# Two blocks as one unit in a Strassen feed-forward: 256 moving rows in the first layer, one load of the second layer's leaves for both

## The chip, the cores and the metric

The kernel runs on one core of one Trainium2 chip. The metric is the device time of one execution in microseconds (us); three runs of the kernel before the change took 1131.85, 1136.12 and 1137.38 us, the median is 1136.12.

## What is computed

Random-feature attention on 8 x 8 heads of 576 rows of 64, then, on its output put together as 4608 rows of 512, a Fourier mix and a feed-forward part, all in float32:

```python
q_p, k_p = (phi(q_s), phi(k_s))              # phi: exp(h - max h) of 128 features
kv = np.einsum('bhsm,bhsd->bhmd', k_p, v)
num = np.einsum('bhsm,bhmd->bhsd', q_p, kv)  # attn_out = num / den
...
u = x + np.real(fft(fft(x, axis=1), axis=2))
un = (u - mean(u)) / np.sqrt(var(u) + 1e-06)
ch = np.maximum(un @ w_ch1, 0.0) @ w_ch2     # 512 -> 2048 -> 512
return u + ch
```

## The kernel before

**Two stages.** The first 423 us hold attention, the Fourier mix, the weights' preparation and the feed-forward of the first 512 rows (four plain blocks of 128). The rest is the feed-forward of eight blocks of 512 rows, numbered j = 0 to 7, and only this is changed.

**A block** is two layers, `un @ w_ch1` (`first_of`, L1466) and `hidden @ w_ch2` (`product_of`, L1833). Each layer is multiplied by two nested steps of the Strassen-Winograd scheme: seven outer products i, each of seven inner leaves n, so 49 leaves a layer and 98 a block. A leaf is four matmuls of 128 x 128 x 128: L1495 in the first layer, with the weights as the stationary and the tokens as the moving operand, and L1892 in the second, with hidden values as the stationary and the leaf `wl` of w2 as the moving operand. Block 0's first layer is an exception: its products other than the first are classical inside (`single`, L1226) and use matmuls of 128 x 256 (L1646).

**Between the leaves.** ScalarE and VectorE take leaf results out of PSUM (L1515 to L1553, L1862 to L1912, L1934), VectorE and GpSimd add hidden cells to each other (`left_sums` L1687, `add` L1455) and make the left sums of the second layer (`add_up` L1848). The hidden values of a block are `hid`: four cells C11, C12, C21, C22, each of 2 x 2 tiles of 128 x 512. Three tiles of `sums`, four of `part`, three of `ur` and twelve of `wl` are handed round.

**Where leaves come from.** Of the first layer's weights, w1 itself, three outer sums `so` (products 5, 6, 3) and the inner sums `w1s` of product 1 stay in SBUF; the three inner sums 5, 6 and 3 of the other six products are made once, kept in DRAM as `w1l` (L1764) and loaded as `wx`, 18 loads of 256 KB a block. The second layer's 49 leaves lie in DRAM as `w2l` and are loaded in every block (L1798), 256 KB each.

**Tokens.** A block's rows are loaded (`u`, L1067), normalized on ScalarE with a little GpSimd, transposed by 32s on VectorE (L1024), stored to DRAM as `turned` (L1032) and fetched in another order as `unT` (L1040). VectorE then makes the outer sums `tt` (L1290) and the inner ones (`token_sums`, L1257). The output rows are read back as `ur` (L1000), the products are added (L1941) and the rows are stored (L1006).

**What sets the order.** Every piece of work is a `Step` of a generator, with its engine, an estimated time, the events it comes after, the buffers it takes and gives, and a due time. A planner, `Listing.run`, lists the steps; the outcome is written down as `PICKS2` and `BANKS2`, one pick a step, so that each engine's queue has a fixed order. All DMAs of this stage but the very last rows go through the SP queue, in that order. `due` (L1990) counts in leaves of 0.9 us, 98 a block.

Of the kernel before, what the change touches and what calls it, by code (L numbers as in the profile page):

```python
# [1 line left out]

# [38 lines left out]
class Clock(NamedTuple):  # L41
# [14 lines left out]
SECOND = Clock(190.0, 0.15, 0.0, 0.1, {}, {}, (PE, ACT, DVE, POOL, SP, NONE), {})  # L56
# [41 lines left out]
    "0w0w0v000u0v0x0y0y0v0y0x0x0v0y0w0z0y0u0t1z0M0u0M1K0K0u1v0Q0N0I0t0W0M0O1L1w0L1U1t0S0Q0R0u010U0S0O0G0G"  # L98
    "0P0T1u0R0s0s000S0O0N0N0T0I0P0z0L0Q0R1R0B0K1P0P0K0K0T0V0I0S0G0U0T0S0U1s0H1r0D0z0x0A1N0w0F0S0P0F0E0O1O"
    "1u0R0v0G0V0V0V0C0S1S0R0L0w0P0S1r0V0M0Q0O0u0y0R0H0L1s0U0P0E0F0M0R1r0D0W0M0#0&0u0T0$0W0M0R0J0L0C0O0V00"  # L100
    "0$0N1q0M0R0G0A0V0u0Z0A0A0Z0R0U0D0S0S0L0G0Z0H0P1Y0F0F0Z0Y1q0$0$0C0D0D0U0T0X0T0#0X0z0V0F0U0V0X0C0B0W0P"
    "0R0U0T0U0v0T0x0Y0N1P0z0u0O0z0I0T0M0N0T0K0A0N0R0x0G0W1F0X0L0I0M0I0x0G0T0U0x0R0R0x0G0I0A0R0G0O0O0E0x0M"
    "0V0U000t0E1G1t0T1L0K0B0O0E0P1L0M0u0K0G1Q0L0R1z0N0C0E0G0E0u0G0D0L1D0N0C1Q0K1O0L0S0M0y0C0T0A0B1L0t0U0U"
    "0T0G0L0R0O0E0R0K0O0M0A0J0L0E1r1z1R0z0K0C0y0y0M0O0M1t0I0A0F0D0C0J0I0E1D0L0C0s1K0H0F0J0J0w0z0I0D0E0H1E"
    "0C0J1E0F0p0M0o0L1K1H1N0M0B0O0G0C0F0J0A0J0J0N0p1G0C1B0H0N0y0E0E0I1H0y1K0G0z0B0L0H0G0N1H0M0H0M0M0M0M1E"
    "0C1J0G0B1I0B1E0y0G0u1E0F0B0D1D1E0u0F0F0y0A0z0y0G0C0J0A0p0D0G0y1G0C0F0z0p0E0u1w0A0D1w0y0y0x0z0F0t0E0B"
    "0F0E1x1v1z1D0C0A0E0E0C0z0t1z0D0C0D1C0B0D0u0x0B0r0x0C0v0A1y0v0u0v0t0t0A0u0o0s0z0A1x0y0C0z0y0A0x0D0A0t"
    "0D0E0E0E0D0A0z0y0z0B0q0s0C0A0x1r0x0z0z1t1D1D0t0s0u0v0r0t0v000u0u0q0r0A1A0x0z0A0s0z0A1q0z0x0y0A0p0v0u"
    "0x0p0p0z0x0x0y0t0w0y0r0q0v0r0q000n0t0E0r0r0n0E0F0A0A0A0G0z0F0p0x0z0L0L0x0z0y0x0H0J0o0w0G0C0G0m0x0v0E"
    "0w0z0A0v0B0x0F0G0A0D0B0I0z0z0G0C0m0E0x0y"  # L110
)
BANKS2 = (
    "5670152675637645127567567560754361752071640532471365062476735"
# [219 lines left out]
def kernel(  # L333
# [53 lines left out]
    w1 = const.tile([128, NDC, DFF], F32, name="w1")  # L387
# [630 lines left out]
    Q = 32  # L1018
    turned = {}

    def by_blocks(j, i, pool, u, h, k):
        yield Step(DVE, 0.69, take=("turn",), give=("u",), makes=("turn", j, i))
        w = pool.tile([P, 4, NDC, Q], F32, name="turn", tag="turn", bufs=1)
        nc.vector.transpose(  # L1024
            out=w[:].rearrange("p g d q -> p d g q"),
            in_=u[:].rearrange("p (d g q) -> p d g q", d=NDC, g=4),
        )
        if (j, h) not in turned:
            turned[j, h] = dram.tile([P, 4, 2, NDC * Q], F32, name=f"turned{j}_{h}")
        t = turned[j, h]  # L1030
        yield Step(SP, 0.55, 6.0, after=(("turn", j, i),), makes=("turned", j, i), give=("turn",), kb=165)
        nc.sync.dma_start(t[:, :, k], w[:].rearrange("p g d q -> p g (d q)"))  # L1032

    def fetched(j, h, dst):
        yield Step(
            SP, 1.7, 3.0, after=(("turned", j, 2 * h), ("turned", j, 2 * h + 1)),
            makes=("unT", j, h), kb=330,
        )
        for g in range(4):
            nc.sync.dma_start(  # L1040
# [4 lines left out]
    def normed(j, pool):  # L1045
        t0 = (NPLAIN * TP + TB * j) // 128

        def paced(i):
            h, k = divmod(i, HT // 128)
            yield Step(  # L1050
                NONE,
                after=events_of(range(t0, t0 + TB // 128)) + ((("first", j - 1, (1, 1, 5, 2)[i]), "y"),),
            )
            yield from norm_of(
                j, t0 + 2 * h, i, pool, None, (h, k), ((("first", j - 1, (6, 2, 7, 3)[i]), "y"),)
            )

        for i in range(TB // 128):
            yield Fork(paced(i), LEAF * (98 * j - 60 + 8 * i))
# [165 lines left out]

    def single(j):  # L1226
# [844 lines left out]
```

## Time and profile before

| what | value |
|---|---|
| median of three runs | 1136.12 us |
| profiled execution, and its span | 1134.51 us, 1132.7 us |
| granted TensorE clock | 1.00 |
| feed-forward of the eight blocks begins at | 423.3 us |
| first-layer leaves, 128x128 f32 matmul records (L1495) | 275 ns each, overlapping |
| second-layer leaves (L1892) | 3136 records, 275 ns each |
| leaf loads | 392 of `wl`, 126 of `wx`, 256 KB each |
| moved by DMA over the span | 258.30 MB, 228 GB/s |

The page of a profile gives busy time by engine, the span in 40 slices, the chain of work that ended last, and the costliest groups of instructions. Matmul records overlap each other, so the time of a leaf is read from the starts of its records, not from their durations.

### The profile page before, as it was taken

Reading aid. Unit: us, or ns where it says so; the run is one execution under the profiler, and the core shown is the slowest. Engines: PE = TensorE matmul, PEld = TensorE weight load, DVE = VectorE, ACT = ScalarE, POOL = GpSimd, SP = SyncE. Lnnn points to the kernel's source line nnn. Section 1 sums busy time; section 2 is a strip of 40 time slices with the busy share of each in tenths; the row PEclk is TensorE's granted clock in tenths of the full one; section 3 lists DMA queues with packets and bytes.
Section 4 is the critical chain, followed back from the end, with each engine's and each line's share of the span. In section 5 each row is a group of like instructions: output and inputs, shape, how many; then the busy total and the mean of one; then the engine's idle time right before and its main releaser. Section 6 shows DMA issues by size and latency. Waiting matters only on the chain.

```text
span 1132.7 us, 34265 instructions
## 1 busy us (share of the span) xinstructions
PE 1116.3 (99%) x13643; PEld 1040.2 (92%) x13643; DVE 867.6 (77%) x1732; ACT 541.7 (48%) x1644; POOL 428.1 (38%) x438
## 2 busy tenths in 40 slices
PE   8999999999999999999999999999999999999998
PEld 7778888879868778999999999999999999999998
DVE  6999899987576655796787778678678678678666
ACT  7888898856535216614424424424423522522311
POOL 2443443654573214613612710710720630540361
PEclk9999999999999999999999999999999999999999
DMA  7856766565763238797797798797698698798576
GB/s 242 224 177 180 224 181 215 170 206 170 222 196 126 93 92 284 211 314 246 227 339 232 219 329 241 213 326 258 202 323 264 210 281 298 214 268 293 184 223 205
DMA packets 187966, 258.30 MB, mean 228 GB/s; under 512 B 52384, under 2 KB 83360, under 8 KB 187808
## 3 DMA queue, kind: packets, MB, share of 16 engines
q1 hardware_dynamic: 187312, 255.85, 73.1%
q8 instruction: 109, 1.79, 0.7%
q14 instruction: 49, 0.40, 0.1%
q10 hardware_dynamic: 496, 0.26, 0.1%
HBM read 212.27 MB, written 47.97 MB: 230 GB/s over the span
## 4 chain that ended last, share of the span: by engine, by line
PE 89%; DVE 4%; ACT 3%; DMA 2%; issue 1%; SPq 0%; DVEq 0%; ACTq 0%
PE banks L1892 28%; PE banks L1495 28%; PE banks L1167 5%; PE banks L658 5%; PE banks L1190 5%; PE banks L564 4%; PE banks L1646 4%; PE banks L692 3%; PE banks L739 2%; PE banks L901 2%; ACT e L618 1%; PE banks L851 1%; DMA unT<-turned 1%; DVE nmx L601 1%; PE banks L861 1%
## 5 line engine op out<-in xcount | busy, mean ns | idle before, releaser
L1892 PE MATMUL banks<-wl,sums 128*128 128x128 f32 x1792 | 218.9, 275 | 0.7 <-DVE sums L1460 0.7
L1892 PEld LDWEIGHTS banks<-wl,sums 128*128 128x128 f32 x1792 | 209.3, 192 | 1.1 <-DVE sums L1460 0.9
L618 ACT ACTIVATE e<-banks,nmx 128x128 f32<-128x128 f32 x576 | 164.3, 423 | 24.3 <-DVE nmx L601 23.7
L1460 POOL TENSOR_TENSOR hid<-hid 128x512 f32<-128x512 f32 x97 | 127.0, 1314 | 119.1 <-ACT hid L1552 66.5
L1892 PE MATMUL banks<-wl,hid 128*128 128x128 f32 x1344 | 170.6, 275 | 0.6 <-DVE part L1870 0.4
L1892 PEld LDWEIGHTS banks<-wl,hid 128*128 128x128 f32 x1344 | 160.2, 192 | 1.1 <-DVE part L1870 0.6
L601 DVE TENSOR_REDUCE nmx<-banks 128x8 f32<-128x1024 f32 (+1 forms) x96 | 89.4, 952 | 18.3 <-PE banks L658 14.2
L1495 PE MATMUL banks<-rx,wx 128*128 128x128 f32 x672 | 88.8, 275 | 0.0
L1865 ACT ACTIVATE s<-banks 128x128 f32<-128x128 f32 x112 | 30.8, 277 | 113.2 <-PE banks L1892 97.7
L1495 PEld LDWEIGHTS banks<-rx,wx 128*128 128x128 f32 x672 | 81.8, 192 | 0.0
L658 PE MATMUL banks<-om,kqT 64*64 64x128 f32 (+1 forms) x2088 | 78.7, 275 | 2.2 <-ACT kv L708 1.9
L1538 DVE TENSOR_TENSOR hid<-banks,s 128x512 f32<-128x512 f32 x72 | 49.7, 691 | 38.9 <-PE banks L1495 36.9
L658 PEld LDWEIGHTS banks<-om,kqT 64*64 64x64 f32 (+1 forms) x2088 | 64.3, 138 | 13.1 <-issue 3.6
L1870 DVE TENSOR_TENSOR part<-banks,s 128x128 f32<-128x128 f32 x112 | 32.1, 288 | 50.0 <-PE banks L1892 48.8
L1520 ACT ACTIVATE s<-banks 128x512 f32<-128x512 f32 x65 | 38.7, 596 | 59.7 <-PE banks L1495 58.6
L1167 PE MATMUL banks<-unT,w 128*128 128x128 f32 x512 | 65.4, 279 | 1.7 <-DVE qeT L578 1.7
L507 POOL TENSOR_TENSOR w<-w,raw 128x512 f32<-128x512 f32 x28 | 37.7, 1356 | 77.6 <-DVE raw L501 77.6
L1442 DVE CUSTOM_DVE_ANT_0 hid<-banks,s 128x512 f32<-128x512 f32 x63 | 43.6, 692 | 27.5 <-PE banks L1495 25.2
L1167 PEld LDWEIGHTS banks<-unT,w 128*128 128x128 f32 x512 | 60.2, 192 | 4.5 <-issue 2.3
L1460 DVE TENSOR_TENSOR hid<-hid 128x512 f32<-128x512 f32 x91 | 61.1, 712 | 3.8 <-ACT hid L1598 3.8
L1518 DVE TENSOR_TENSOR s<-banks,hid 128x512 f32<-128x512 f32 x70 | 48.4, 691 | 19.0 <-PE banks L1495 16.7
L1941 POOL TENSOR_TENSOR ur<-ur,part 128x512 f32<-128x512 f32 x21 | 26.8, 1281 | 95.4 <-ACT part L1934 91.6
(200 smaller groups left out, 2387.4 us busy)
## 6 DMA issues: line engine op xcount, KB each, us to landing
wl<-w2l SPq DMA_DIRECT2D x392, 256.0 KB
wx<-w1l SPq DMA_DIRECT2D x126, 256.0 KB
raw<-in_moe_w_ch_dram SPq DMA_DIRECT2D x32, 512.0 KB
kq<-in_k_dram SPq DMA_DIRECT2D x32, 288.0 KB
kq<-in_q_dram SPq DMA_DIRECT2D x32, 288.0 KB
vd<-in_v_dram SPq DMA_DIRECT2D x32, 288.0 KB
u<-us SPq DMA_DIRECT2D x36, 256.0 KB
ur<-us SPq DMA_DIRECT2D x36, 256.0 KB
```

Of the source, the lines that this page charges most:

```text
L564: nc.tensor.transpose(ps[:, (j - j0) * 128 : (j - j0 + 1) * 128], src(j), ident[:])
L601: nc.vector.tensor_reduce(nmx[:, :, 0:num], pps[:, :, 0 : MF * num].rearrange("p b (c m) -> p b c m", m=MF), axis=AX.X, op=ALU.max, negate ...
L618: nc.scalar.activation(out=e[:, c + (i if num == 1 else 0), :], in_=pps[:, i, MF * c : MF * c + MF], func=AF.Exp, bias=nmx[:, i, c : c + 1],)
L658: nc.tensor.matmul(pps[cols, c, MF * m : MF * m + MF], lhsT=kqT[rows, j, cols], rhs=om2[rows, :],)
L1167: nc.tensor.matmul(hp[:, 0:TP], lhsT=w1[:, dc, 128 * fc : 128 * fc + 128], rhs=unTs[key][:, dc, :], start=(dc == 0), stop=(dc == NDC - 1),)
L1190: nc.tensor.matmul(yp[:, 0:DM], lhsT=hs[fc][:, 128 * i : 128 * i + 128], rhs=w2[:, fc, :], start=(fc == 0), stop=(fc == NFC - 1),)
L1460: eng.tensor_tensor(out=o, in0=l, in1=r, op=op)
L1495: nc.tensor.matmul(ps[:, P * f : P * f + P].rearrange("f (b q) -> f b q", q=Q), lhsT=left[:, P * f : P * f + P], rhs=right, start=start an ...
L1518: nc.vector.tensor_tensor(out=s[:], in0=ps, in1=cell_of(addend, f, t), op=ALU.add)
L1538: nc.vector.tensor_tensor(out=o, in0=ps, in1=kept[saved][:], op=ALU.add)
L1646: nc.tensor.matmul(cell.rearrange("f t (b q) -> f t b q", q=Q), lhsT=w[:, d, col : col + 128], rhs=right[:, :, d].rearrange("f (t b) q -> ...
L1892: nc.tensor.matmul(ps[:, 0:128], lhsT=left[:, f], rhs=wls[j, i, n][:, f], start=start and f == 0, stop=(f == 3), skip_group_check=True,)
```

## The change

Blocks 0 and 1 stay as they are. Blocks 2 and 3, 4 and 5, 6 and 7 become three units (`WIDE`, `head`, `unit`).

- *First layer.* A leaf's moving operand is 256 rows, 128 of each of the two blocks, and its result is two 128 x 256 tiles: two matmuls in place of four. Each outer product runs in two passes g, one for each half of a leaf's weight columns. All 49 leaves are read from DRAM, in halves of 1 KB a partition (`w1x`), two halves a load.
- *Stores.* For that, the leaves that stayed in SBUF are stored too: 31 more stores of 256 KB (`w1_stored`), in blocks 0 and 1. The 18 stores that were there go in the same layout.
- *Second layer.* The two blocks' products run interleaved, and one load of a leaf serves both.
- *Buffers.* The second half of a unit's hidden cells takes the place of w1 once that has been read for the last time; the normalized tokens take that of `so5` and `so6`, spare rows and parts that of `so3`, spare token sums that of `rx` and `w1s`.
- *Tokens.* The eight norms of a unit are paced over the first layer before it, and fetched in 64 KB pieces.
- *Plan.* `PICKS2` and `BANKS2` are new, `SECOND`'s rate is 240 for 190, and due times and biases go by 196 leaves a unit.

```diff
+    WIDE = 2
+    def wide(j):
+        return j >= WIDE
...
-            left, right = weights_of(j, i, n), tokens(j, i, n)
-            for f in range(4):
+            left, right = weights_of(j, i, n, g), tokens(j, i, n)
+            for f in range(4 * P // span):
                 nc.tensor.matmul(
-                    ps[:, P * f : P * f + P].rearrange("f (b q) -> f b q", q=Q),
+                    ps[:, span * f : span * f + span].rearrange("f (b q) -> f b q", q=Q),
                     lhsT=left[:, P * f : P * f + P],
                     rhs=right,
...
+    def w1_store(i, n, after, at):
+        yield Step(SP, 0.45, 2.5, after=after, kb=128, makes=("w1x", i, n), bias=at)
+        w = weights_of(0, i, n)
+        nc.sync.dma_start(leaf_in(i, n), w.rearrange("p (g n) -> p g n", g=2))
...
     def load_leaves():
-        for j in range(NTB):
-            for i in twice(j):
+        for j in HEADS:
+            for i in ORDER1 if wide(j) else ():
+                for m in range(7):
+                    after = tuple(("w1x", i, PARTS[k % 7]) for k in (2 * m, 2 * m + 1))
+                    yield Step(SP, 0.45, 2.6, take=("wl",), after=after, kb=165, makes=("wx", j, i, m),
+                               bias=due(j, 0, i) + LEAF * 2 * m - 14)
+                    wx = late.tile([128, 2, GW // 2], F32, name="wxw", tag="wl", bufs=NWL)
+                    nc.sync.dma_start(wx[:], w1x[i][2 * m : 2 * m + 2].rearrange("l p n -> p l n"))
+                    wxs[j, i, m] = wx
...
+    def factor(j, i):
         c = {1: C11, 2: C21, 4: C22, 7: C12, 6: C22, 5: C11, 3: C21}[i]
+        if wide(j):
+            a = P * (j - head(j))
+            return lambda t, f: hw[c][:, f, t, :, a : a + P]
...
                 nc.tensor.matmul(
                     ps[:, 0:128],
                     lhsT=left[:, f],
-                    rhs=wls[j, i, n][:, f],
+                    rhs=wls[head(j), i, n][:, f],
...
+            for i in order(j):
+                for k in unit(j):
+                    yield Step(NONE, take=("set",))
+                    yield Fork(product_of(k, i, cells[k]), due(k, 1, i))
...
+    def widened():
+        yield Step(
+            NONE,
+            after=tuple(("w1x", i, n) for i in ORDER1 for n in PARTS)
+            + tuple((("first", WIDE - 1, i, 0), "leaves") for i in ORDER1),
+        )
+        old = hid[:].rearrange("p c f t n -> p (c f t n)")
+        new = const.tile([128, 8 * DFF // 2], F32, name="hx", tag="w1")[:]
+        n = new.shape[1] // 2
+        for h in (old, new):
+            for k in range(2):
+                hw.append(h[:, n * k : n * k + n].rearrange("p (f t k n) -> p f t k n", f=2, t=2, k=4))
```

## The prediction, made before the change was run

> **What bounds the kernel now.** I read the page's header and slices first, then the chain that ended last, then who waited for whom in the second half, then windows cut at the block and layer boundaries.
>
> ```profile
> span 1132.7 us, 34265 instructions
> PE 1116.3 (99%) x13643; PEld 1040.2 (92%) x13643; DVE 867.6 (77%) x1732; ACT 541.7 (48%) x1644; POOL 428.1 (38%) x438
> ```
>
> TensorE is busy 99% of the span. Which part of that can move is seen from the chain (start, length, what) and from all that TensorE waited for between 423 us, where block 0 begins, and the end:
>
> ```profile
> 519.37 37.52 PE banks L1495 x336
> 561.36 32.16 PE banks L1892 x288
> ```
>
> ```profile
> PE banks L1892 <- DVE sums L1460: 0.9, 2, 0.7
> PE banks L1892 <- DVE part L1870: 0.4, 1, 0.4
> ```
>
> In 710 us TensorE waits 1.3 us in all. The eight blocks are a row of leaves, end to end. One f32 matmul leaves two records, so a leaf of four 128-column matmuls is 8 records: 32.16 / 288 x 8 = 0.893 us in the second layer, 37.52 / 336 x 8 = 0.893 us in the first. A block is 98 leaves, 87.5 us; seven of them are 612.8 us, which is where the span's second half goes. So only two things can move the time: the length of a leaf, and new waits.
>
> The second resource to look at is DMA. Columns: stretch, its length, busy us of PE, PEld, DVE, ACT and POOL with counts, clock, DMA share, GB/s. These are block 0's second layer, block 1's first and second, and the last block's first.
>
> ```profile
> 471.00:515.00 44.00, 43.27 (x376) 42.77 (x375) 38.18 (x70) 11.43 (x40) 9.60 (x9) 1.00 0.99 312
> 515.00:559.00 44.00, 44.00 (x397) 44.00 (x396) 29.59 (x56) 21.89 (x44) 25.49 (x27) 1.00 0.69 216
> 559.00:602.60 43.60, 43.60 (x393) 43.60 (x392) 35.30 (x67) 10.93 (x36) 7.41 (x9) 1.00 0.96 307
> 1040.30:1084.00 43.70, 43.70 (x394) 43.70 (x394) 29.48 (x58) 13.11 (x25) 17.91 (x14) 1.00 0.58 183
> ```
>
> Every second layer runs the DMA engines at 0.95 to 1.00 and TensorE still doesn't wait; first layers use about 0.70. DMA is the next bound, a few per cent away.
>
> **What goes: the width of first-layer matmuls.** From block 2 on a first-layer leaf is two matmuls of 256 moving rows in place of four of 128. Block 0's classical products already run 128x256 f32 matmuls with the same strided runs of 32 (L1646); in the timeline two groups start 8.63 us apart:
>
> ```profile
> 440.63 8.80 PE L1646 MATMUL banks<-tt,so 128*128 128x256 f32 x40
> 449.26 3.62 PE L1646 MATMUL banks<-unT,w 128*128 128x256 f32 x16
> ```
>
> 8.63 / 40 = 0.2158 us a record, four records a leaf: 0.863 us. The saving is 0.893 - 0.863 = 0.030 us a leaf. Three units of 2 x 49 leaves are 294: **8.8 us less TensorE time**, and nothing else shortens TensorE, since second-layer matmuls keep their form.
>
> A rule on this: the Trainium skill, "TensorE: Matmul & The Clock Gate", section "Wait — 56ns, not 53.3ns?", gives start to start as N/2.4 GHz plus about 2.5 ns a matmul. If a record is two passes, that makes 111.7 ns at 128 columns, which the trace agrees with (111.7), and 218.3 ns at 256, where the trace has 215.8; by the rule, as an estimate, the saving would be 5.9 us.
>
> **What is added or moved, off TensorE's path.**
>
> Evictions: the same number of 128x512 ones, since a unit's leaf gives 2 x 256 columns. Token sums: 28 DVE instructions of 128x256 in a unit replace 56 of 128x128. Between L1257's 287 ns at 128 and L1290's 688 ns at 512 elements that is about 420 ns: 11.8 us for 16.1 us, DVE gains 4 us a unit, which isn't on the path. Second-layer sums now read four runs of 128 floats a stride apart: L1257 reads runs of 32 at 287 ns and L1870 unbroken 128 at 288 ns, so strides cost nothing here.
>
> Steady DMA: a unit needs 49 first-layer and 49 second-layer loads of 256 KB where two blocks needed 36 and 98. The first kind comes in 1 KB packets. In the trace's single packets 2 KB take 84 ns in the median and 101 in the mean, 1 KB 46 and 69 (48 in the last output stores, 60 to 82 in the scattered unT loads), 512 B 27 and 28. A first-layer load of 256 packets on 16 engines is nearest to the weight loads, unbroken in DRAM: 46 x 101/84 = 55 ns, 0.88 us. A unit's first layer then moves 49 x 0.88 = 43.1, eight u loads, eight ur loads and eight output rows at 0.81 (19.4) and eight turned stores at 0.90 (7.2): 70 us in 84.6, a share of 0.82; its second layer, 49 x 0.81 and 32 small unT loads of 64 KB at 0.28, 49 us in 87.5: 0.56. Both are under the 0.96 that runs now without waits.
>
> DMA in blocks 0 and 1: here the change loads what is nearly full. The queue's first instruction of this stage starts at 424.4, so all of it falls between 424 and 602.6, the end of block 1. Free by the shares (0.77, 0.99, 0.69, 0.96): 11.0 + 0.4 + 13.6 + 1.7 = 26.7 us. Added, with 48 ns for 1 KB stores and 55 for loads: 31 more stores of weight leaves, 256 x 48 / 16 = 0.77 us each, 23.8; 18 stores and 18 loads that now go in 1 KB packets, 0.5; block 3's four u loads, four turned stores and unT loads, 3.2 + 3.6 + 3.5 (55 ns) = 10.3; the first four loads of block 2's own leaves, 3.5. Gone: ten of block 2's old loads, issued from 592.66 on, 8.1. Sum 30.0 us for 26.7 free: 3 us over. With 46 ns throughout it is 25, inside what is free; with 69 ns it is 52, 26 us over. Twelve load buffers are a lead of 12 x 0.893 = 10.7 us, which takes up the 3 us. I take **1.5 us of new waits** for loads that come out of turn, and keep 0 and 16 (26 less 10.7) as the ends.
>
> A rule on this: the Trainium skill, "HBM Reference", section "Specifications (TRN2)", says that a core streaming alone reaches about 425 GB/s, bounded by its 16 DMA engines; by it the roughly 58 MB of the two blocks (48.1 by the windows' GB/s, 9.6 added) would need 136 us of 179 and nothing could wait. The trace doesn't show that rate: 301 to 312 GB/s in full second layers, 365 in the best 10 us.
>
> New waits on buffers: the unit's hidden cells C21 and C22 lie where w1 was, so their first write waits for every store of a w1 leaf and for block 1's last first-layer leaf. That write is on DVE, and every later eviction stands behind it; it comes with the second product, some 12 us into the unit, when the stores should be long done. The stores wait on SP for weight sums, and the loads stand behind them there. Sums buffers stay three while two products run interleaved, so the fourth product's first sum waits for a leaf of the first and then has about 3.6 us for a 0.7 us add; today's cost of such sums is the 0.9 us above. I take 0.5 us, between 0 and 3.
>
> The end: now 5.1 us pass between 1127.6, where the unbroken row of leaves ends, and the span's end. Its last steps are:
>
> ```profile
> 1127.98 1.16 PE L1892 MATMUL banks<-wl,hid 128*128 128x128 f32 x8 [0.39 <-DVE part L1870]
> 1129.17 0.29 DVE L1824 TENSOR_TENSOR ur<-ur,banks 128x128 f32<-128x128 f32 x1 [0.72 <-PE banks L1892]
> 1129.49 0.54 SPq L1011 DMA_DIRECT2D out_dram<-ur  x1
> ```
>
> Afterwards block 6's last product ends one leaf before block 7's, so its eviction (0.28), its 0.69 us add and then two row stores of 256 KB stand near the end, where now 64 KB go out in halves. Two stores are 1.6 us of transfer where 128 KB now take 0.4: 1.2 us later. The interleaving covers the 0.39 us wait. Net +0.8, between -0.5 and +2.
>
> Sum: -8.8 + 1.5 + 0.5 + 0.8 = -6.0 us. The profiled execution took 1134.51 us (span 1132.7, 1.8 around it), so 1128.5; it lies 1.6 under the median of 1136.12, so in the median **1130 us**, 0.5% faster.
>
> **Rivals.**
>
> 1. *The stores choke blocks 0 and 1 (slower).* If 1 KB packets cost 69 ns or more among neighbours, and the stores pile up in block 1 beside eight norms, second-layer loads queue behind them: 16 us of TensorE waits, spread over 471 to 620. The point from which it decides is about 60 ns a packet. For it: 0.99 and 0.96 shares, and a 2 KB mean 20% over its median. Against it: TensorE didn't wait at 0.99, and the output's 1 KB stores took 48 ns. 1136.1 - 8.8 + 16 + 1.1 = 1144 us.
> 2. *Half of that (no change that can be measured).* At 60 ns the excess is about 15 us, less the lead, 4 to 6 of waits: 1133 to 1134.
> 3. *Everything hides.* No new wait, the end as now: 1136.1 - 8.8 - 0.4 = 1127.
> 4. *The change doesn't do what it says*: 256-column leaves run no faster among LDWEIGHTS from freshly loaded leaves. L1646 reads resident weights; but L1495's loaded and resident forms are alike at 275 ns, so this is unlikely: 1137 us.
> 5. *A fixed cost a column pass takes back part of it*: on the line through 111.7 ns at 128 columns and 429.1 at 512 (L1190, 13.73 us for 32 records) 256 columns take 217.5 a record, a leaf 0.870: 6.9 less, 1132. The Trainium skill's rule above is of this form and makes it 1133.
>
> **How the numbers follow.** My forecast (waits of 0 to 3 us) 0.42, everything hides 0.13, half choked 0.17, choked 0.22, no faster leaf 0.03, the fixed cost 0.03. A measurement of this kernel tells about 0.5%, 5.7 us, from no change; the limits are 1130.4 and 1141.8. Faster: the third rival whole, two thirds of the forecast's own spread (1127 to 1132), a part of the runs' scatter (1131.85 to 1137.38 now): 0.48. Same: the rest of the forecast, the second, fourth and fifth rivals and the mild end of the first: 0.34. Slower: 0.18. The range reaches from 1125 (everything hides, less 2 for scatter) to the choked case, 1144.
>
> **What would show it.** Right: first-layer records of 128x256 at 0.216 us, from 87.5 + 87.5 = 175 us a pair of blocks to 169.2 a unit; TensorE waits after 423 us still under 4 us; DMA share near 1 in blocks 0 and 1 and 0.55 to 0.85 later. Wrong: TensorE waits on loads (L1892 or the new leaf line behind wl) before the first unit; waits on sums in the second layer; a store that ends the chain more than 2 us later than now. What would break the forecast outright is a unit boundary where TensorE waits for tokens or for hidden cells, of which the present trace shows nothing.

## The result, and the profile after

The changed kernel takes 1177.6 us in the median of four runs (1175.68 to 1186.3), where the kernel before takes 1135.57 in four: **a ratio of 1.039, 95% interval 1.033 to 1.045**. It is slower, by 42 us. The prediction was 1130 us, with 1125 to 1144 as its range, so it was wrong, in sign too. The profiled execution took 1186.3 us, its span 1184.5.

The page's header for the changed kernel, the counterpart of the first lines shown of before:

```profile
span 1184.5 us, 31492 instructions
PE 1126.1 (95%) x12467; PEld 1010.2 (85%) x12467; DVE 878.0 (74%) x1689; ACT 541.2 (46%) x1644; POOL 376.0 (32%) x397
```

TensorE is busy for 95% in place of 99%. What it waited for from 420 us on (what waited, total us, times, longest) has many releasers now, where before it had two and 1.3 us:

```profile
PE banks L1605 <- ACT banks L1637: 8.2, 1, 8.2
PE banks L2052 <- DMA wl<-w2l: 8.1, 4, 5.7
PE banks L1605 <- ACT s L1630: 6.2, 5, 1.8
PE banks L1605 <- DVE hid L1535: 6.2, 3, 3.9
PE banks L1605 <- DVE hx L1535: 3.5, 2, 1.8
PE banks L2052 <- DVE more L2028: 2.3, 2, 2.0
```

L1605 is the first layer's leaf now, L2052 the second layer's. Most of the waits are behind evictions on ScalarE (L1630, L1637) and behind VectorE instructions that come after these, all in the first layer. With the rest of that answer they make 43 us. VectorE stands still with ScalarE: in block 1 it was idle for 9.2 us ahead of a norm's transposition (L1030), until ScalarE had written the normalized `u`. One row of ScalarE's own waits says what ScalarE was doing meanwhile; the second line is the same row in the kernel before:

```profile
ACT junk L1096 <- DMA u<-us: 78.4, 26, 7.3
```

```profile
ACT junk L1076 <- DMA u<-us: 9.6, 7, 2.3
```

`junk <- u` is the first activation of a norm. It waits in ScalarE's queue for the rows `u`, and the evictions of TensorE's results stand behind it. The chain of waits in the second unit shows the pattern. Between these pieces lie the norm itself and a few leaves; the last line is the first layer of the last unit, which has no norms beside it:

```profile
821.95 8.34 DMA u<-us
830.79 8.61 DMA u<-us
...
844.43 7.23 DMA u<-us
...
857.62 7.58 DMA u<-us
...
870.89 8.01 DMA u<-us
...
1007.89 78.56 PE banks L1605 x364
```

The planner issues a load one product before its norm and takes it to land after 3.0 us; in the units it takes 6.6 to 8.6, and every one of their 16 norms waits. The last line also holds the change's promise: 78.56 / 364 x 4 = 0.863 us a leaf, as predicted.

The windows (length, busy PE, PEld, DVE, ACT and POOL with counts, clock, DMA share, GB/s) of block 0's second layer, block 1's two layers, the first unit's two layers, and the last unit's first:

```profile
465.20:515.90 50.70, 46.74 (x385) 45.28 (x385) 38.72 (x67) 16.13 (x49) 12.09 (x13) 1.00 1.00 294
515.90:580.10 64.20, 51.22 (x410) 50.46 (x409) 34.50 (x72) 28.76 (x61) 19.91 (x29) 0.87 0.84 266
580.10:639.30 59.20, 49.64 (x403) 48.02 (x402) 38.19 (x67) 13.25 (x44) 13.08 (x14) 0.94 0.84 258
639.30:724.00 84.70, 80.94 (x374) 69.45 (x373) 56.66 (x95) 40.92 (x81) 36.11 (x42) 1.00 0.74 206
730.40:819.60 89.20, 88.22 (x775) 87.53 (x775) 77.43 (x143) 20.96 (x74) 5.11 (x7) 1.00 0.62 188
1003.00:1090.00 87.00, 87.00 (x424) 77.13 (x423) 58.15 (x93) 28.26 (x50) 35.94 (x28) 1.00 0.62 191
```

Block 1 takes 64.2 and 59.2 us for what took 44 and 43.6. Its mean granted clock is 0.87 and 0.94: after each of its three long waits TensorE runs at half clock for about 5 us (the last section has the windows).

Throughout I use one measure that leaves the first stage out: the time from block 0's first matmul to the last matmul, split where the second layers end. (Neighbouring blocks overlap a little, so two neighbours are read together.) By it the eight blocks took 707.1 us before and 758.5 after. The six blocks that became three units should have fallen from 524.0 to 515.2, by the 8.8 us of the prediction; they rose to 539.8. Blocks 0 and 1, which the change leaves as they are, rose from 183.1 to 218.7.

### The profile page after: what moved, and what is told of

Read it like the earlier page. It is cut to its first block, busy times and chain, and to the rows that moved or that the text cites. A ratio compares the mean times of both kernels' runs of the same rounds, so it can differ in the third digit from the quotient of the medians.

```text
span 1184.5 us, 31492 instructions
## 1 busy us (share of the span) xinstructions
PE 1126.1 (95%) x12467; PEld 1010.2 (85%) x12467; DVE 878.0 (74%) x1689; ACT 541.2 (46%) x1644; POOL 376.0 (32%) x397
## 5 line engine op out<-in xcount | busy, mean ns | idle before, releaser
L2052 PE MATMUL banks<-wl,sums 128*128 128x128 f32 x1792 | 222.2, 277 | 3.6 <-ACT s L2023 2.7
L2052 PEld LDWEIGHTS banks<-wl,sums 128*128 128x128 f32 x1792 | 212.3, 193 | 5.4 <-ACT s L2023 3.3
L2052 PE MATMUL banks<-wl,hid 128*128 128x128 f32 x768 | 102.0, 280 | 10.6 <-DMA wl<-w2l 7.4
L2052 PEld LDWEIGHTS banks<-wl,hid 128*128 128x128 f32 x768 | 94.7, 195 | 12.2 <-issue 7.0
L1605 PE MATMUL banks<-unw,wxw 128*128 128x256 f32 x384 | 93.5, 380 | 0.7 <-ACT s L1630 0.7
L1605 PEld LDWEIGHTS banks<-unw,wxw 128*128 128x128 f32 x384 | 72.3, 190 | 11.2 <-ACT s L1630 1.1
L1605 PE MATMUL banks<-rx,wxw 128*128 128x256 f32 x288 | 71.6, 381 | 7.2 <-DVE hx L1535 3.5
L2052 PE MATMUL banks<-wl,hx 128*128 128x128 f32 x576 | 75.5, 278 | 2.1 <-DVE part L2028 2.1
L1605 PE MATMUL banks<-ttw,wxw 128*128 128x256 f32 x288 | 70.8, 381 | 3.3 <-ACT s L1630 3.3
L2052 PEld LDWEIGHTS banks<-wl,hx 128*128 128x128 f32 x576 | 70.1, 194 | 3.1 <-DVE part L2028 2.7
L1605 PEld LDWEIGHTS banks<-rx,wxw 128*128 128x128 f32 x288 | 54.0, 190 | 16.4 <-DVE hx L1535 4.3
L1605 PEld LDWEIGHTS banks<-ttw,wxw 128*128 128x128 f32 x288 | 54.2, 190 | 11.9 <-ACT s L1630 4.1
L1630 ACT ACTIVATE s<-banks 128x512 f32<-128x512 f32 x65 | 38.4, 591 | 52.4 <-PE banks L1605 46.9
L2028 DVE TENSOR_TENSOR part<-banks,s 128x128 f32<-128x128 f32 x100 | 28.9, 290 | 44.4 <-PE banks L2052 43.7
```

The costliest lines, as they stand in the source:

```text
L1605: nc.tensor.matmul(ps[:, span * f : span * f + span].rearrange("f (b q) -> f b q", q=Q), lhsT=left[:, P * f : P * f + P], rhs=right, start ...
L1630: nc.scalar.activation(out=s[:], in_=ps, func=AF.Copy)
L2028: nc.vector.tensor_tensor(out=part[:, t, 128 * m : 128 * m + 128], in0=ps[:, 0:128], in1=saved[with_][:], op=ALU.add,)
L2052: nc.tensor.matmul(ps[:, 0:128], lhsT=left[:, f], rhs=wls[head(j), i, n][:, f], start=start and f == 0, stop=(f == 3), skip_group_check=True,)
```

## The experiments

All edits are to the changed kernel but one (m1_mirror). "Beside it" is the kernel before on the same chip. h2_spread and h3_lead2 were timed four times, i1_spread17 and j3_two ten times; the other times are single executions. The four of the changed kernel lie 10.6 us apart, and the profiled one is the slowest, 8.7 us over their median. So a few microseconds between two single runs mean something only where a wait in the trace goes with them. Eighteen runs:

| run | us | beside it | blocks 0, 1 | the other six | TensorE waits from 420 us |
|---|---|---|---|---|---|
| before, profiled | 1134.51 | | 183.1 | 524.0 | 1.3 |
| after, profiled | 1186.3 | | 218.7 | 539.8 | 43.3 |
| a1_apart | 1154.85 | 1130.72 | 210.9 | 519.7 | 23.7 |
| a2_ahead | 1176.05 | 1130.72 | 218.9 | 532.9 | 40.5 |
| a3_both | 1157.76 | 1130.72 | 212.2 | 520.1 | 27.6 |
| a4_split | 1149.89 | 1130.72 | 203.0 | 521.7 | 18.1 |
| c1_late | 1162.14 | 1132.05 | 216.2 | 521.4 | 29.2 |
| m1_mirror | 1134.95 | 1132.05 | 184.5 | 525.2 | 3.3 |
| b1_steps | 1153.34 | 1132.05 | 205.4 | 522.5 | 22.8 |
| c3_all | 1153.23 | 1132.05 | 206.7 | 520.4 | 21.8 |
| d1_wide4 | 1158.21 | 1132.05 | 193.8 | 536.2 | 20.7 |
| e1_poolfetch | 1144.17 | 1132.05 | 197.3 | 522.4 | 15.5 |
| e2_idlestores | 1156.53 | 1132.05 | 192.4 | 521.6 | 12.3 |
| e3_both | 1151.64 | 1132.05 | 186.6 | 522.4 | 7.7 |
| g1_replanned | 1151.6 | 1131.9 | 204.5 | 522.5 | 20.3 |
| h2_spread | 1152.62 | 1131.9 | 199.5 | 527.0 | 17.7 |
| h3_lead2 | 1153.61 | 1131.9 | 199.5 | 528.6 | 16.4 |
| i1_spread17 | 1141.24 | 1133.45 | 184.5 | 530.5 | 10.0 |
| i2_bunch17 | 1145.87 | 1133.45 | 193.7 | 526.0 | 12.7 |
| j3_two | 1136.72 | 1131.86 | 185.7 | 526.3 | 8.0 |

With units from block 4 on, the other six should take 518.1. In c3_all, d1_wide4 and the runs from g1 on, part of the output differs from the reference's by far more than rounding, for a reason that isn't known. TensorE runs the number of matmuls there that the form of the kernel asks for, so their times are read, but none of them is a kernel to use.

### First question: is it ScalarE behind u, or the stores?

**a1_apart**: the units' norms read a constant and no longer the loaded rows, so nothing on ScalarE waits for `u`.

```diff
+            x, w = u[:], u
+            if wide(j):
+                x, w = ident[:].unsqueeze(1).to_broadcast([P, 4, 128]), ur1
```

> Of the changed kernel (1177.6 us). The norms of the units' blocks no longer read what the u load brings: ScalarE reads a constant tile instead and writes the norm into another tile; the u loads themselves stay (the rows of blocks 2 to 7 are therefore not the input's). Order and all DMAs are unchanged. Theory A (ScalarE's queue stands behind u loads that take 7 to 8 us, and what it should take out of PSUM comes late): block 1 falls from 123 us to about 100, the three first layers of the units from 92 to 86, no wait on ACT junk by DMA u is left; 1140 to 1150 us. Theory B (the stores overload DMA in blocks 0 and 1, and leaf loads come late): block 1 keeps most of its 36 us excess; 1165 to 1172.

Blocks 2 to 7 fall from 539.8 to 519.7 us, near the 515.2 that the prediction wanted; the kernel gains about 23 us against the median. Theory A holds for the units. It misses block 1, which falls only from 118.0 to 113.5 us where 100 were expected. There another queue takes ScalarE's place: VectorE waits 6.5 us to transpose the next norm, until the store of the tokens before it has freed their tile, and TensorE waits 5.3 us behind VectorE:

```profile
542.22 0.71 DVE L1030 STREAM_TRANSPOSE turn<-ur 128x512 f32<-128x512 f32 x1 [6.52 <-DMA turned<-turn]
544.75 1.65 PE L1609 MATMUL banks<-rx,w 128*128 128x128 f32 x6 [5.32 <-DVE hid L1539]
```

**a2_ahead** takes the 31 stores out of SP's queue and out of this stage:

```diff
+    nc.scalar.dma_start(w1x[1].rearrange("l p n -> p l n"), flat1[...])
+    for i in INNER:
+        for k, n in enumerate((1, 2, 7, 4)):
+            nc.scalar.dma_start(leaf_in(i, n), ...)
-        nc.sync.dma_start(leaf_in(i, n), w.rearrange("p (g n) -> p g n", g=2))
```

> Of the changed kernel. The 31 added stores of weight leaves are issued from ScalarE's queue before the eight blocks begin, all at once, with other data (raw w1 in place of sums, so first-layer weights of the units are not the input's); SP's queue has none of them. Theory A: only the waits on leaf loads go (8 us of waits in block 0 and 1 and the half clock after them), u loads still take 7 us: 1160 to 1170. Theory B: block 1 falls to 95 us or less: 1145 to 1152.

and **a3_both** does both.

> Both edits together: norms don't read the u load, and the 31 stores come ahead of the stage. If A and B hold all of the excess, TensorE waits less than 5 us after 423 us and the time is about 1136 - 9 + 2 = 1129 us. If a third cause is there (token chain, buffers, order of the unit), it stays over 1140.

Both are spoilt in block 0. There ScalarE stood behind the stores that had been moved to its own queue:

```profile
ACT banks L1637 <- DMA w1x<-w: 28.9, 1, 28.9
```

TensorE lost 12.8 us by it. Only the direction is of use: block 1 fell from 118.0 to 107.1, so the stores cost something there too, but the units keep their loss as long as norms read `u` (532.9) and lose it when they don't (520.1). How much the stores cost stayed open.

The traces of the changed kernel and of a2_ahead show one way in which they cost. In the changed kernel SP issues the first load `u` of block 1 behind stores, and ScalarE is at that norm 0.5 us later; it then waits 7.3 us, and TensorE 8.2 behind it, its longest wait:

```profile
527.84 1.24 SPq L1087 DMA_DIRECT2D u<-us  x2
```

```profile
535.64 0.63 ACT L1096 ACTIVATE junk<-u 128x512 bf16<-128x512 f32 x1 [7.33 <-DMA u<-us]
```

In a2_ahead, without the stores in SP's queue, ScalarE comes to that norm 9.0 us after its load was issued and doesn't wait.

### Second question: why does u land late?

**a4_split** changes nothing but the form of the units' `u` loads:

```diff
-            nc.sync.dma_start(u[:], rows[block[1]])
+                for n in range(4):
+                    nc.sync.dma_start(u[Q * n : Q * n + Q], rows[block[1], n])
```

> Of the changed kernel. Each u load of the units' blocks is four DMAs of 32 rows in place of one of four groups of 32 rows; nothing else. If the 7 to 8 us of a u load are its own (its packets going through few of the 16 DMA engines), they fall to 3 to 5 us and the time by 10 to 20 us, 1157 to 1168. If they are the line of other transfers ahead of it, they stay, and three more issues of 0.5 us each on SP change little: 1175 to 1180.

1149.89 us, 7 us under the range expected, and units at 176.2, 172.4 and 173.0 in place of 184.5, 182.2 and 173.0. The load's rows are four groups of 32. The Trainium skill, "DMA: Bandwidth & Descriptors", section "Why a DMA increments its semaphore by 16 and not by 1", says that a transfer is spread over as many of 16 engines as divide the slowest dimension on both sides: four engines by that rule, and 16 for each of the four pieces. The trace agrees: by its semaphore events each of the 24 loads of the changed kernel has five (one 0.9 to 1.7 us after the issue, then four between 5.7 and 10.0 us, the last of them the landing), and each of the 96 pieces of a4_split has 16. From the first issue to the last landing the four pieces take 3.4 to 6.0 us, 3.9 in the median. One norm of the second unit in the changed kernel, issue on SP and first activation on ScalarE (start, length, what, in brackets the idle time before it and its releaser):

```profile
857.62 0.57 SPq L1087 DMA_DIRECT2D u<-us  x1
```

```profile
865.22 0.63 ACT L1096 ACTIVATE junk<-u 128x512 bf16<-128x512 f32 x1 [4.00 <-DMA u<-us]
```

and one in a4_split, with no wait:

```profile
851.94 1.97 SPq L1089 DMA_DIRECT2D u<-us  x4
```

```profile
856.13 0.61 ACT L1100 ACTIVATE junk<-u 128x512 bf16<-128x512 f32 x1
```

**c1_late** leaves the load as it is and tells the planner that it lands after 7.5 us and not 3.0:

```diff
-        yield Step(SP, 0.42, 3.0, take=("u",), kb=256)
+        yield Step(SP, 0.42, 7.5 if block else 3.0, take=("u",), kb=256)
```

> Of the changed kernel (1177.6 us; with u loads in four parts 1149.9). One number of the planner: a u load of these norms is expected to land 7.5 us after its issue, not 3.0; the u load itself stays one DMA. If ScalarE's queue waits on u loads only because the order has the norm stand where the plan thinks them landed, ScalarE's waits on u fall from 78 us to under 15 and the time to that of the four-part load, 1145 to 1155. If the load's slowness costs in another way (its buffer is held longer), it stays over 1160.

1162.14 us: the units are repaired (521.4), block 1 isn't (118.4), since its first steps are in the written order and the new time can't move them. ScalarE still waits 40.2 us on `u`, where under 15 were expected, so in total the run misses; the units show that the place of the norm in the order is enough to hide a slow load.

**m1_mirror** puts the suspect alone into the kernel before: from block 3 on, a norm's load is issued one product ahead, as in the units.

```diff
-  (("first", j - 1, (1, 1, 5, 2)[i]), "y")
+  (("first", j - 1, ((1, 1, 5, 2) if j < 3 else (1, 5, 2, 7))[i]), "y")
```

> The kernel before, with one thing of the change: from block 3 on a norm's u load is issued one product ahead of its first activation on ScalarE, as in the units, and no longer up to three products ahead. Theory U (the lead of one product is shorter than the 7 us that the load takes, and ScalarE's queue stands behind it): ScalarE waits 3 to 7 us on u in most norms of blocks 3 to 7, where it waited 2.3 us in one norm of four; slower than before by 8 to 18 us, 1140 to 1150. Rival (a product of 128-column leaves gives the same lead and only the unit's doubled traffic makes it late): within 3 us of before.

The theory missed its number; the rival's was right (2.9 us over the kernel beside it). The 15 loads that it moves took 5.4 to 7.5 us to land, but:

```profile
ACT junk L1076 <- DMA u<-us: 26.7, 18, 2.8
PE banks L1495 <- ACT banks L1527: 1.1, 1, 1.1
```

ScalarE waited 26.7 us, never more than 2.8 at a time, and TensorE 3.3 us in all. But the lead wasn't the same. ScalarE came to these 15 norms 4.7 to 6.2 us after the issue of their load, 5.7 in the median; to the 16 norms of the units in the changed kernel it came 2.6 to 7.9 us after it, 4.4 in the median. The loads themselves landed 7.0 us after the issue here and 7.7 there, in the median. So of the units' longer waits, up to 4.9 us, some two thirds are the shorter lead, as an estimate from these medians; one third, the slower load, is all that the rival's reason, the unit's doubled traffic, can hold. Waits of under 3 us cost TensorE next to nothing here, where those of the units and of block 1, up to 7.3 us, cost it much. That results find room in PSUM during the short ones is argued, not shown.

### Third question: what is left in block 1?

After a4_split 20 us of the loss stand in blocks 0 and 1. SP's queue in a4_split shows a candidate, and TensorE's timeline the price:

```profile
588.63 9.53 SPq L1048 DMA_DIRECT2D unw<-turned  x16
598.26 13.38 SPq L1952 DMA_DIRECT2D wl<-w2l  x21
```

```profile
601.26 2.05 PE L2056 MATMUL banks<-wl,hid 128*128 128x128 f32 x8 [5.79 <-DMA wl<-w2l]
```

SP issues 16 of the 64 KB fetches in 9.5 us, and the leaf loads come behind them. From here on every kernel has a4_split's loads. **b1_steps** made each fetch a step of its own, so that leaf loads could go between:

```diff
-            SP, 3.4 if wide(j) else 1.7, 3.0, ...
+            SP, 0.45 if wide(j) else 1.7, 3.0, ...
...
+                    if g or t:
+                        yield Step(SP, 0.45, 3.0, ...)
```

> Of the kernel with u loads in four parts (1149.9 us). The eight small unT fetches of a half are eight steps with due times of their own, where one step issued all eight in a row. Theory: SP's queue issues 16 fetches in 9.5 us ahead of second-layer loads of block 1, which is the 5.8 us wait on a leaf load and the half clock behind it: they go, block 1 falls from 106 to 98 us, 1140 to 1144 us. Rival (DMA itself is full there, the wait moves elsewhere): 1147 to 1151.

**c3_all** added c1's edit, with a landing time of 5.0 us, to that, and **d1_wide4** began the units at block 4 too (`WIDE = 4`).

> Of the changed kernel: u loads in four parts, the plan's landing time for them 5.0 us, fetches as steps of their own. If the two queues (ScalarE behind u, SP behind the fetches) are all but the stores' share of the excess, TensorE waits under 8 us after 423 us, the units take 172 us each and block 1 90 to 95: 1130 to 1138 us, against 1130.7 for the kernel before on that chip. If the stores' DMA share still costs 10 us in block 1: 1138 to 1145.

> The same three edits, and units only from block 4 on: blocks 2 and 3 run as in the kernel before, and the 31 stores have two more blocks of time. Saves 196 leaves' 0.030 us, 5.9 us, at best. If the crowding of DMA before the first unit is the rest of the excess, nothing waits: 1125 to 1131 us, faster than the three edits alone. If not, it is slower than they by the 2.9 us that one unit saves.

All three missed. The planner still issued most of the fetches together (15 in 9.1 us in c3_all), so none of them tested the idea. **e1_poolfetch** did, by another queue:

```diff
-            SP, 3.4 if wide(j) else 1.7, 3.0, after=
+            POOL if wide(j) else SP, 8.0 if wide(j) else 1.7, 3.0, after=
...
-                    nc.sync.dma_start(
+                    nc.gpsimd.dma_start(
```

> The u loads of the units go as four DMAs of 32 rows, as in a4_split, and the fetches of the transposed tokens (32 of 64 KB in a unit) are issued from GpSimd's queue and no longer from SP's. Theory S (what is left in block 1 is SP issuing 16 fetches in one go, 9.5 us, with the leaf loads behind them): the 5.8 us wait on wl near 601 us goes, with the half clock behind it; block 1 from 106 us to 96, time about 1140 where the kernel before takes 1131. Theory D (it is the DMA share that 31 more stores take): no change against a4_split, block 1 between 104 and 108 us, 1148 to 1152.

The 5.8 us wait is gone (all waits on `wl` are 1.8 us, the longest 1.0); block 1 takes 98.4 us for 106.2, the time is 1144.17. Theory S holds for that part, 4 us short of its number. What is left in block 1 are waits of 3.6 and 3.0 us behind evictions. **e2_idlestores** and **e3_both** take the other suspect away, without and with e1's edit: the stores are left out of blocks 0 and 1.

```diff
-        nc.sync.dma_start(leaf_in(i, n), w.rearrange("p (g n) -> p g n", g=2))
+        for i in ((), (1, 6, 5), (2, 7), (3, 4))[j]:
+            nc.scalar.dma_start(w1x[i].rearrange("l p n -> p l n"), w1[...])
```

> Split u loads as in a4_split, and no store of a weight leaf in blocks 0 and 1: the leaves that the units read are filled from the raw w1 before 423 us, so the units' first layer multiplies by other weights than the reference's. Theory D (the stores' DMA share): block 1 goes from 106 to 88-95 us, time 1133 to 1140 where the kernel before takes 1131. Theory S (16 fetches in a row on SP): the wait on wl near 601 us stays, block 1 between 100 and 106, 1144 to 1150.

> Both edits, so split u loads, fetches from GpSimd's queue, and no store of a weight leaf in blocks 0 and 1 (other weights in the units' first layer). If u loads, fetches on SP and stores are all there is: block 1 at 87 to 90 us, units at 172 to 174, 1122 to 1130, at or under the kernel before's 1131, which is what the prediction expected. If it stays over 1136, there is a further cause in block 1 that none of the three theories has.

Their times are no use, since the filling made the first stage 14 to 15 us longer (block 0 begins at 437 us, in after at 422.5); the stage is. In e2_idlestores block 1 takes 97.0 us, between the two theories' ranges. From block 0 on e3_both takes 709.0 us where e1_poolfetch takes 719.6 and before 707.1: the stores cost 10.6 us, and so they do without e1's edit (714.1 against a4_split's 724.7). u, fetches and stores together are 49.5 of the 51.4 us by which the changed kernel is over the kernel before; 10.7 are missing to the 698.3 that were due. ScalarE comes to block 1's first norm 9.0 us after the issue of its load again, where in e1_poolfetch it is 1.0, and the two waits of 3.6 and 3.0 us are gone. What remains are waits of TensorE of 7.7 us:

```profile
PE banks L2056 <- DMA wl<-w2l: 3.0, 4, 1.1
PE banks L2056 <- DVE more L2032: 2.3, 2, 2.0
PE banks L2056 <- DVE part L2032: 1.4, 3, 0.7
```

### Fourth question: the stores' transfers, or their place in SP's queue?

These have e1_poolfetch's fetches as well. **g1_replanned** dropped the written order, so stores went out earlier; **h2_spread** began units at block 4 and put 21 stores one behind each first-layer product of blocks 1 to 3; **h3_lead2** loaded `u` two products ahead. The lines that spread the stores in h2_spread:

```diff
+                    if k > 9:
+                        b, p = divmod(k - 10, 7)
+                        after += ((("first", 1 + b, ORDER1[p], 0), "y"),)
```

> As e1_poolfetch (split u loads, fetches from GpSimd's queue), but the order written down for this stage is left out and the planner orders it anew: the 31 stores then go out as soon as they may, 22 of them in block 0 and 9 in block 1. If the stores' DMA share costs the 11 us that e3_both puts on it, an earlier bunch moves the waits from block 1 into block 0 and the time stays at 1140 to 1148; if only their place among the leaf loads on SP costs, it may come down to 1132 to 1136.

> As g1_replanned, with the units beginning at block 4 (two units) and 21 of the 31 stores spread, one behind each first-layer product of blocks 1 to 3. Theory D (the stores fit where the DMA engines have room): no store bunch is left, TensorE waits after 423 us come down to 3 to 6 us; two units gain 5.9 us; 1128 to 1134 where the kernel before takes 1131 to 1132. If waits of 10 us or more stay in blocks 0 and 1, the stores weren't it: 1138 or more.

> As h2_spread, with a norm's u load issued two products ahead and no longer one. ScalarE's waits on u in the units (about 1 us a norm with the split load) go; if they still reach TensorE, 1 to 3 us less than h2_spread; if not, the same within 1 us.

Inconclusive: without the written order block 0 alone takes 109 to 114 us, whether 22 or 10 of the stores fall in it, and that hides the rest. In timed runs h2_spread is 1.017 of before (1.014 to 1.020), h3_lead2 1.018 (1.016 to 1.021). **i1_spread17** and **i2_bunch17** have their units from block 4 on too, keep the written order through block 0, and differ only in when the 17 later stores go.

> Split u loads, fetches from GpSimd's queue, units from block 4 on, the written order kept through block 0 (which the new plans of h2_spread and h3_lead2 lost 10 to 15 us in) and planned anew from block 1 on; the 17 stores of block 1 go one behind each first-layer product of blocks 1 to 3. Theory D (the stores' DMA share): block 1 under 90 us, TensorE waits after 423 us under 6 us, two units gain 5.9 us, so 1126 to 1133 where the kernel before takes 1131 to 1132. Theory S (place in SP's order): as i2_bunch17 within 3 us.

> As i1_spread17, but the 17 stores go as soon as they may, within 11 us of block 1. Theory D: block 1 between 92 and 100 us, 5 to 10 us slower than i1_spread17. Theory S: as i1_spread17 within 3 us.

Block 1 takes 92.8 us with the bunch and 86.2 with the stores spread; before it was 85.8. SP's queue in i2_bunch17 has the 17 stores within 17 us, and behind them the first `u` load of block 1's norms; then come ScalarE's wait for it and TensorE's for ScalarE:

```profile
521.19 3.41 SPq L1920 DMA_DIRECT2D w1x<-so  x4
525.62 0.57 SPq L1091 DMA_DIRECT2D u<-us  x1
```

```profile
532.61 0.63 ACT L1100 ACTIVATE junk<-u 128x512 bf16<-128x512 f32 x1 [6.51 <-DMA u<-us]
534.72 2.08 PE L1609 MATMUL banks<-tt,so 128*128 128x128 f32 x8 [4.38 <-ACT banks L1641]
```

In i1_spread17 that load leaves earlier, and nobody waits for it:

```profile
510.77 1.33 SPq L1091 DMA_DIRECT2D u<-us  x2
```

The 4.4 us are TensorE's only wait in block 1 of i2_bunch17, with some 5 us at half clock behind them. The load itself takes 7.0 us, no longer than elsewhere, and no leaf load is waited for. So the loss in block 1 is the bunch's place in SP's queue, ahead of a load that ScalarE needs, which is theory S's cause at theory D's size; that the stores' transfers choke the DMA engines isn't what the trace shows. Nor are spread stores free: blocks 2 and 3, where 12 of them go, take 181.5 us in i1_spread17 and 178.7 in i2_bunch17, with 5.8 and 2.9 us of waits, and all in all the two are 4.6 us apart.

Both missed their ranges for the whole: i1_spread17 is slower, 1.0065 of before (1.0045 to 1.0084), where 1126 to 1133 us were expected; its other six blocks take 530.5 where 518.1 were due. **j3_two** moved the 17 stores into blocks 1 and 2, so that block 3, which carries the first unit's eight norms, has none, and the planner takes a `u` load to land after 5.0 us. Against i1_spread17:

```diff
-                        b, p = divmod(k - 12, 7)
+                        b, p = divmod(k - 14, 9)
...
-        yield Step(SP, 0.42, 3.0, take=("u",), kb=256)
+        yield Step(SP, 0.42, 5.0 if block else 3.0, take=("u",), kb=256)
```

> As i1_spread17, with the list of PSUM banks cut where the new order begins (i1_spread17 and i2_bunch17 kept five banks of the old order, so a few of their sums start in banks that hold other numbers), the 17 stores spread over the first layers of blocks 1 and 2 alone, so that block 3 has its DMA room for the first unit's eight norms, and the planner told that a unit's u load lands after 5.0 us. Theory D with u loads as the other cause: the 5.8 us that TensorE waited in blocks 2 and 3 of i1_spread17 fall to 1 to 3, so 1131 to 1137; at the kernel before's 1131 to 1133 at best, since two units gain 5.9 us and blocks 0 and 1 keep 1 to 2 us of waits. If the waits of i1_spread17 come from elsewhere: 1138 to 1143.

1136.72 us, 1.0045 of before (1.0029 to 1.0061): the shortest time of all versions of the change, still no faster than before, and with part of the output wrong. (That part is wrong by as much as in i1_spread17, so the list of banks, which the expectation names, isn't the reason.) Of the versions with the right output, e1_poolfetch is the fastest, 1144.17 us in one execution. j3_two's time is at the upper end of the expected range, and TensorE's waits in blocks 2 and 3 fall from 5.8 to 3.0 us, also the upper end; 2.5 of these are on `wl`. Where the rest of its 8 us over 518.1 comes from I leave open.

## Why the prediction was wrong, point by point

**The failed step is the one that costs the change "off TensorE's path".** It has the eight norms of a unit only as DMA bytes: "block 3's four u loads, four turned stores and unT loads". It asks what these move and never which engine waits for them in order. Two queues were missed, ScalarE's behind `u` and SP's ahead of it. The rows are profiled executions, and the second starts from the changed kernel's slowest:

| from the first matmul of block 0 to the last | us |
|---|---|
| before | 707.1 |
| narrower first layer, as predicted and as leaves measure it | -8.8 |
| `u` loads in one piece (after against a4_split) | +33.8 |
| SP's leaf loads behind fetches (a4_split against e1_poolfetch) | +5.1 |
| the stores (e1_poolfetch against e3_both) | +10.6 |
| what e3_both still loses against 698.3 | +10.7 |
| after | 758.5 |

The terms were taken away one after another, so each holds what it brings in that order; the fetches and the stores bring the same in the other order (a4_split, e2_idlestores, e3_both: 10.6, then 5.1). Of the second term 18.1 us are the units', and a1_apart and c1_late reach them (20.1 and 18.4) by other edits: that ScalarE stands behind `u` there is shown. The other 15.7 lie in blocks 0 and 1, where a1_apart, without any wait of ScalarE on `u`, gets back 7.8; for the rest that way is not shown, and 8.7 us lie between the profiled execution and the median. Against the median a4_split gains 27.7 us, in one execution.

- *The width of matmuls*: right. A leaf takes 0.863 us, and a unit that nothing holds up 172 where two blocks took 175.1. (The 169.2 us a unit among the prediction's signs is a slip: by its own leaves it is 84.6 + 87.5 = 172.1.)
- *ScalarE behind `u`*: in no term and no rival, and it was in the profile of before. There the fourth norm of each block waited 0.9 to 2.3 us, with its load issued 7.3 to 8.5 us ahead, so the load's time could be read as 7 to 8.5 us:

```profile
896.66 0.52 SPq L1067 DMA_DIRECT2D u<-us  x1
```

```profile
905.15 0.63 ACT L1076 ACTIVATE junk<-u 128x512 bf16<-128x512 f32 x1 [2.28 <-DMA u<-us]
```

  The change gives all eight norms of a unit that lead and had me ask only about bytes.
- *SP behind fetches*: the prediction counts 32 fetches as 64 KB each at 0.28 us of transfer, and not as 32 instructions on SP at 0.6 us.
- *DMA in blocks 0 and 1*: "I take 1.5 us of new waits", with ends of 0 and 16. The stores cost 10.6, inside the ends and seven times the value, but by another way, so that the ends hold it is luck. Where the stores lie in the changed kernel (424 to 475 and 505 to 545 us), 1 KB packets took 46 ns in the median and 49 in the mean, as the prediction had it (48) and far from the 60 or 69 that the first two rivals need; with the fetches off SP's queue TensorE waits 1.8 us for `wl` in block 1. What the traces show the stores hold up is the issue of the `u` load behind them: 0.5 us ahead of its norm in the changed kernel, 9.0 in e3_both. Whether their transfers cost something besides stays open.
- *Steady DMA of a unit*: 0.82 and 0.56 predicted, 0.62 to 0.75 and 0.62 measured. TensorE waited for no leaf load in the units; its 8.1 us on `wl` all lie in blocks 0 and 1.
- *Buffers*: 0.5 predicted, between 0 and 3. In e3_both waits on parts and evictions of the second layer are 2.4 us, and another 2.3 are on evictions into spare parts (`more`), 2.0 of them at once in the last unit, 62 us before the last matmul ends: 4.7 together, over the upper end.
- *The end*: predicted +0.8, between -0.5 and +2. From the last matmul to the span's end it is 3.6 us as before.
- *What would break the forecast*: the prediction named the unit's boundary, where TensorE would wait for tokens. It broke a layer earlier, where the tokens are made: the tokens were in time, and the engine that made them was late for its other work.

## What to carry to other kernels

For every instruction that a change moves or multiplies, write down whose queue it waits in and what stands behind it there; bytes and busy time don't show it, as ScalarE was 46% busy when it cost TensorE some 20 us in the units alone. Ask the same of the engine that issues: a store that nobody waits for can hold up the load behind it. Read a load's time from issue to first use out of the trace, by its access pattern, and not from its size: the same 256 KB took mostly 7 to 8 us in one piece of four groups and about 4 in four pieces. Where a sum is the small difference of two large ones, its value is a range.

## What the runs showed of the hardware

**A long wait costs TensorE more than itself.** The timeline of the changed kernel and the window behind the wait, with the next window for comparison:

```profile
541.25 2.08 PE L1605 MATMUL banks<-tt,so 128*128 128x128 f32 x8 [8.21 <-ACT banks L1637]
```

```profile
541.00:546.00 5.00, 4.75 (x23) 4.75 (x24) 3.01 (x7) 2.69 (x5) 1.46 (x2) 0.53 0.98 315
546.00:551.00 5.00, 5.00 (x47) 5.00 (x47) 2.35 (x5) 1.69 (x3) 2.48 (x2) 1.00 0.83 265
```

23 records in 5 us, then 47: the granted clock is half for nearly 5 us, which costs some 2.5 us on top of the wait. Waits of 3.90 and 5.69 us were followed by a clock of 0.50 too, and so was the 2.01 us at 1118.55, for 3.4 us (18 records in 3.3 us, then 32). Of the 60 us that after takes over 698.3, waits are 43, and the half clock behind these four is some 9, an estimate from 4.5, 5.3, 5.5 and 3.4 us at half speed. The Trainium skill, "TensorE: Matmul & The Clock Gate", section "Wait — 56ns, not 53.3ns?", has a cold array run at half its warm rate, and the records agree.

**Stores issued from ScalarE's DMA queue held ScalarE up for 28.9 us** in a2_ahead: 24 of 256 KB in a row took 28.7 us to issue, 1.2 each. On SP's queue in the changed kernel the same stores took 0.4 us each in the median, but four in a row took 4.45, 1.1 each, so it is the row that is dear and not ScalarE's queue as such.

**A load's semaphore tells how many engines it went through**: five events for `u` in one piece, 16 for each quarter, and 6.6 to 10.0 us against 3.4 to 6.0 until it had landed.
